# The first channel product of the last batch as seven half-size products for eight

## The chip, the cores and the metric

The kernel runs on one core of a Trainium2 chip. The metric is device time in microseconds (us) of one execution; the median of several runs is compared. The engines are named as in the profile: PE (TensorE), with PEld for its weight loads, DVE (VectorE), ACT (ScalarE), POOL (GpSimd) and SP (SyncE, which here issues DMAs). Matmuls write PSUM, eight banks of 128 partitions x 512 f32; only PE, ACT and DVE work on it here. All else lies in SBUF.

## The reference

Sliding-window attention with four sink tokens (batch 4, 8 heads, 768 tokens, head size 64), followed by a block that mixes tokens and channels (512 channels):

```python
x   = attention(q, k, v).transpose(0, 2, 1, 3).reshape(4, 768, 512)
a1  = alpha1 * x + beta1
tok = einsum("ts,bsd->btd", w_tok, a1)
u   = x + lam * tok
a2  = alpha2 * u + beta2
ch  = maximum(a2 @ w_ch1, 0) @ w_ch2        # 512 -> 2048 -> 512
out = u + lam * ch
```

The change touches `a2 @ w_ch1` of batch 3, the last one.

## The kernel before, in words

Work is in f16 with sums in f32. Each batch goes through attention (24 steps of head pairs and windows), token mixing (`tok`, six tiles of 128 tokens x 512 channels, each six matmuls of 512 columns, then a DVE add into x, which now holds u, L867, and a cast to f16 on ACT or POOL), a transpose of u by DMA (`uTx`: SP issues six DMA transposes, L919; then eight affines by alpha2 and beta2, one for each 128 channels and each half of the tokens, on ACT, L884, or DVE, L886), the first channel product and the second one. The attention of a batch is interleaved with the channel products of the one before it; batch 3's products at the end have nothing beside them but the end of batch 2's.

**First channel product** (`mlp1`): h is made transposed, 2048 hidden channels as 16 tiles of 128, 768 tokens as 2 chunks of 384. Each of the 32 tiles `h_chunk_fi` is one PSUM bank (pool d, four banks) and four matmuls of 384 columns (L940) over the 512 input channels; then one relu into hT, on ACT (L946) or DVE (L948).

**Second channel product** (`prod`, batches 1 to 3): here the 2x2 block product of hT (tokens by hidden halves) with w_ch2 (hidden by channel halves) already is done as seven products P1 to P7 for eight, by Winograd's form of Strassen's method. Four sums of w_ch2 (L972) and four sums of hT (`h_sums`, S1 to S4, L998 to L1001) are made ahead. A product's tile of 128 tokens x 256 channels is eight matmuls of 256 columns (L1057). The results are gathered by DVE in x (L1070) and, where two outputs share a sum, in an SBUF tile pt (L1088), which is added to x in 512 columns (L1096) and in 256 (L1093). At the end x goes out by DMA (L1076).

**What sets the order.** Every piece of work is a task. Four tables, written out, hold for all tasks their order (ORDER), engine (ENGINES), the buffer that each tile gets from its pool (HOMES) and some idle matmuls (IDLES); `Plan.emit` (L54 to L74) issues the tasks in this order. Each engine then runs its own instructions strictly in that order, and waits by semaphores are set where a tile is written after others have read or written it, for the tile as a whole. Of PSUM's eight banks four are single (pool d); pool S is two tiles of two banks, used in attention for scores. Pool E (six SBUF tiles) holds the exponentials, n16 (four) the f16 copies of q and k, wst (four) w_ch2 on its way in; all these are free by batch 3's end.

Of the kernel before, what the change touches and what calls it, by code (L numbers as in the profile page):

```python
# [77 lines left out]
def kernel(  # L78
# [119 lines left out]
    for r in range(NR):  # L198
# [91 lines left out]
    )  # L290
    ENGINES = (
        "3313134433443333444444444444444433334443111211211212021212021203331121211210210200201210"
# [7 lines left out]
        "2032121312121312104210421040001210421042104000121212120212121212121202120202021202121202"  # L300
        "0202020112120202020212020112021212121211111212121212121213121112131214214214210214214044"
        "4404404404433333304040404043404040202010121203012121312010121213320103212131203012121312"
        "0321213321213121042104210410002104213421341010202021202120212120212020202020212020212120"
        "202020112020212021202020112020210202142141111212121212121211121112131210210210214210210"
    )
    HOMES = (
        "145602340010102001213310200221013302203140101100511203013044215120821000003331a501103130"
# [4 lines left out]
        "0021102210121102223200511310123320031102032021035337572302312010320101420152002210101311"  # L312
        "162103012154110041003020b005101119102307200030023123011223130032122313100100121232070302"
        "1202002102135312330203"
    )
    IDLES = (
        (46, 0, 67), (90, 1, 25), (109, 3, 2), (166, 1, 4), (162, 0, 1),
# [528 lines left out]
    pch = {}  # L846

    def tok(p, b, ti):
        pt = Buf("S" if (b, ti) == (0, 5) else "d", None, None, f"tok{b}_{ti}")
        bx = x[b, ti]  # L850

        def bank():
            return pt.t[:, 0] if pt.kind == "S" else pt.t
        bu = u16[b, ti] = Buf("u16", None, None, f"u16_{b}_{ti}")
        hs = [xh[b, si] for si in range(NR)]

        def mm(sis):
            def f(e):
                for si in sis:
                    nc.tensor.matmul(  # L860
                        bank(), wtokT[:, si, ti * P : (ti + 1) * P], hs[si].t,
                        start=(si == 0), stop=(si == NR - 1))
            return f

        def ua(e):
            xf = bx.t.rearrange("p h d -> p (h d)")
            nc.vector.tensor_add(xf, xf, bank())  # L867
# [64 lines left out]
    def mlp1(p, b, chk, fi):  # L932
        if fi == 0:
            hT[b, chk] = Buf("hT", None, None, f"hT{b}_{chk}")
        bh, bu = hT[b, chk], uT[b, 0]
        ph = Buf("d", [P, NTOK], FP32, f"h{b}_{chk}_{fi}")

        def mm(e):
            for c in range(NC):
                nc.tensor.matmul(  # L940
                    ph.t, w1f[:, c, fi * P : (fi + 1) * P],
                    bu.t[:, c, chk * NTOK : (chk + 1) * NTOK], start=(c == 0), stop=(c == NC - 1))

        def relu(e):
            if e == ACT:
                nc.scalar.activation(bh.t[:, fi, :], ph.t, AF.Relu)  # L946
            else:
                nc.vector.tensor_scalar_max(bh.t[:, fi, :], ph.t, 0.0)  # L948
# [261 lines left out]
    for b in range(B):  # L1210
        w0 = STEP * b
        if b == 0:
            seq = [("tok", ti) for ti in range(3)] + [("uT", 0, 0), ("uT", 0, 1)]
            seq += [("tok", ti) for ti in range(3, NR)]
            m1 = []
            for qd in range(4):
                for chk in range(2):
                    m1 += [("m1", chk, fi) for fi in range(4 * qd, 4 * qd + 4)]
            m1.insert(3, ("uT", 1, 0))
            m1.insert(5, ("uT", 1, 1))  # L1220
        else:
# [3 lines left out]
        seq += m1  # L1225
        if b in STRASSEN:
# [4 lines left out]
            i = seq.index(("m1", 1, 8))  # L1231
# [21 lines left out]
        for i, (what, *args) in enumerate(seq):  # L1253
# [8 lines left out]
            {"tok": tok, "uT": uTp, "m1": mlp1, "m2": mlp2, "hs": h_sums, "pr": prod}[what](p, b, *args)  # L1262
            if b and what == "tok":
                uTx(p + 0.3, b, *args)
        if b + 1 == STRASSEN[0]:
# [68 lines left out]
```

## Time and profile before

| | |
|---|---|
| time, median of three runs | 254.27 us (254.3, 254.27, 253.2) |
| profiled execution, its own time | 253.3 us |
| its span | 251.5 us |
| matmul busy in the span | 245.2 us, 98% |
| DVE, ACT, POOL busy | 193.7, 131.5, 107.9 us |
| batch 3's first product on PE | 207.76 to 230.53, with a few tiles of the second product of batch 2 and 3 in between |
| batch 3's second product on PE | to 247.94 |

Of the profile this document shows: the share of busy time of each engine; the chain that ended last; groups of instructions ("L940 PE MATMUL h<-uT,w1f 128*128 128x384 f16 x512 | 89.3, 326 | 0.1" is: line, engine, operation, out<-in, shapes, how many | busy us, mean ns of one | idle us of the engine just before them, and what ended it); timelines (start us, us, engine, line, operation, out<-in, how many, and in brackets the idle time before with its releaser); and windows (for a stretch of time its length, then the busy time of each engine with its instructions, TensorE's granted clock as a share of full speed, the DMA share and GB/s). In a timeline a piece of several matmuls is listed up to its modelled end, which lies a little behind the start of the next. A line is that of the program's source; a helper's line (L155, L157: copies and casts) serves many places.

### The profile page before, as it was taken

The page shows a single profiled execution, that of the slowest core. Times are in us where ns is not written, and L with a number is a line of the kernel's source. Part 1 is how long each engine was busy: PE and PEld are TensorE (multiplying, and loading weights), DVE is VectorE, ACT ScalarE, POOL GpSimd, SP SyncE. Part 2 cuts the span into 40 slices and gives each one's busy share as a digit, 9 for nine tenths or more (in the row PEclk, how much of TensorE's full clock was granted, in tenths as well). Part 3 has the DMA queues.
Part 4 walks back from the last instruction along what each step waited for, and adds up shares of the span by engine and source line. Part 5 has one row for each costly group of instructions (what it writes and reads, how often), then busy time and mean ns, then how long its engine had stood idle before and what let it go on. Part 6 is the DMA issues. An engine that isn't in the chain of part 4 may idle for free.

```text
span 251.5 us, 5513 instructions
## 1 busy us (share of the span) xinstructions
PE 245.2 (98%) x2167; PEld 160.2 (64%) x2167; DVE 193.7 (77%) x401; ACT 131.5 (52%) x218; POOL 107.9 (43%) x126
## 2 busy tenths in 40 slices
PE   8899999999999999999999999999999999999994
PEld 7654655575555444566777676567677676567883
DVE  6898987778788976688889995677689985119883
ACT  2389935788985125687750545556660235543000
POOL 8728724986866516442872040065563130000010
PEclk9999999999999999999999999999999999999999
DMA  6999999999999997796489264420000147100006
GB/s 206 212 262 346 222 183 292 361 357 285 219 208 220 231 198 163 166 257 150 108 171 183 55 148 136 126 65 0 3 0 3 21 77 234 46 0 3 22 3 229
DMA packets 86129, 38.79 MB, mean 154 GB/s; under 512 B 73540, under 2 KB 80460, under 8 KB 86104
## 3 DMA queue, kind: packets, MB, share of 16 engines
q1 hardware_dynamic: 66976, 28.85, 48.2%
q10 hardware_dynamic: 15384, 6.32, 10.5%
q0 software_dynamic: 3744, 3.28, 8.3%
q8 instruction: 17, 0.28, 0.5%
q14 instruction: 8, 0.07, 0.1%
HBM read 29.91 MB, written 6.29 MB: 144 GB/s over the span
## 4 chain that ended last, share of the span: by engine, by line
PE 90%; ACT 4%; DVE 3%; issue 1%; DVEq 0%; ACTq 0%
PE h L940 32%; PE P L1057 22%; PE tok L860 12%; PE ch L1125 8%; PE pv L726 4%; PE S L625 4%; PE idle L148 2%; PE tp L515 1%; ACT wt L822 1%; ACT E L647 1%; DVE qkT L157 1%; PE S L620 1%; PE tp L512 1%; PE pv L719 1%; DVE lb_b L1175 1%
## 5 line engine op out<-in xcount | busy, mean ns | idle before, releaser
L940 PE MATMUL h<-uT,w1f 128*128 128x384 f16 x512 | 89.3, 326 | 0.1
L940 PEld LDWEIGHTS <-w1f 128*128 128x128 f16 x512 | 48.4, 98 | 31.9 <-issue 2.0
L946 ACT ACTIVATE hT<-h 128x384 f16<-128x384 f32 x77 | 36.7, 492 | 34.5 <-PE h L940 30.7
L948 DVE TENSOR_SCALAR hT<-h 128x384 f16<-128x384 f32 x51 | 27.4, 552 | 23.7 <-PE h L940 23.3
L1057 PEld LDWEIGHTS <-hT 128*128 128x128 f16 x408 | 39.3, 98 | 7.2 <-DVE hT L1000 0.7
L647 ACT ACTIVATE E<-S 128x1024 f16<-128x1024 f32 (+1 forms) x39 | 37.9, 1002 | 6.8 <-PE S L625 5.7
L770 POOL TENSOR_TENSOR tm<-x,la_b 128x512 f32<-128x512 f32 x18 | 24.7, 1372 | 22.2 <-DVE xh L773 12.0
L860 PE MATMUL tok<-xh,wtokT 128*128 128x512 f16 x144 | 33.2, 379 | 0.0
L1057 PE MATMUL P<-w2f,hT 128*128 128x256 f16 x216 | 26.8, 273 | 0.0
L155 ACT CAST u<-x 128x512 f16<-128x512 f32 x17 | 10.3, 616 | 28.3 <-DVE x L867 27.3
L1093 POOL TENSOR_TENSOR x<-x,pt 128x256 f32<-128x256 f32 x4 | 3.8, 961 | 46.0 <-DVE pt L1088 46.0
L1070 DVE TENSOR_TENSOR x<-x,P 128x256 f32<-128x256 f32 x45 | 18.0, 417 | 6.8 <-PE P L1057 6.0
L1057 PE MATMUL P<-w2s,hT 128*128 128x256 f16 x192 | 23.3, 273 | 0.0
L860 PEld LDWEIGHTS <-wtokT 128*128 128x128 f16 x144 | 13.8, 98 | 14.8 <-issue 0.2
L1125 PE MATMUL ch<-w2f,hT 128*128 128x512 f16 x96 | 22.7, 379 | 0.0
L752 DVE TENSOR_TENSOR x<-pv,rec 128x256 f32<-128x256 f32 x48 | 20.4, 425 | 1.7
L155 ACT CAST n<-nat 128x768 f16<-128x768 f32 x20 | 16.2, 830 | 7.9 <-DMA out_dram<-x 4.8
L867 DVE TENSOR_TENSOR x<-x,tok 128x512 f32<-128x512 f32 x24 | 16.0, 681 | 4.5 <-PE tok L860 4.3
L726 PEld LDWEIGHTS <-E 128*128 128x128 f16 x328 | 15.2, 97 | 4.9 <-issue 1.1
L726 PE MATMUL pv<-vfs,E 128*128 128x65 f16 x328 | 17.7, 193 | 0.0
L587 POOL TENSOR_SCALAR_AFFINE_SELECT E<-E 128x512 f16<-128x512 f16 x12 | 8.8, 753 | 17.9 <-ACT E L647 17.9
L157 POOL CAST vfs<-vnat 128x512 f16<-128x512 f32 x18 | 13.5, 752 | 4.3 <-PE pv L726 4.2
(133 smaller groups left out, 340.1 us busy)
## 6 DMA issues: line engine op xcount, KB each, us to landing
wst_w<-in_moe_w_ch_dram SPq DMA_DIRECT2D x8, 512.0 KB, 7.4
nat<-in_q_dram SPq DMA_DIRECT2D x10, 384.0 KB, 4.3
nat<-in_k_dram SPq DMA_DIRECT2D x10, 384.0 KB, 8.1
vnat<-in_v_dram SPq DMA_DIRECT2D x14, 256.0 KB, 6.2
out_dram<-x SPq DMA_DIRECT2D x12, 256.0 KB, 3.4
wtn<-in_moe_w_tok_dram SPq DMA_DIRECT2D x6, 384.0 KB, 4.8
out_dram<-x ACTq DMA_DIRECT2D x9, 256.0 KB, 4.3
w1f<-in_moe_w_ch_dram POOLq DMA_DIRECT2D x4, 512.0 KB, 10.2
```

The costliest lines, as they stand in the source:

```text
L155: nc.scalar.copy(o, i)
L647: nc.scalar.activation(eT.t, pS.t[:, :, 0 : n * w].rearrange("p e (i w) -> p e i w", i=n), AF.Exp, scale=scale)
L726: nc.tensor.matmul(po.t[:, hl, :], eT.t[:, e_, off + i, c : c + P], vf[j][:, h, :], start=(r < 2 and n == 0), stop=(n == len(parts) - 1 an ...
L752: nc.vector.tensor_mul(bx.t[:, 4 * G : 4 * G + 4, :], po.t[:, :, 0:D], rec.t.to_broadcast([P, 4, D]))
L770: engine[e].tensor_mul(bt.t, bx.t.rearrange("p h d -> p (h d)"), la1_b)
L860: nc.tensor.matmul(bank(), wtokT[:, si, ti * P : (ti + 1) * P], hs[si].t, start=(si == 0), stop=(si == NR - 1))
L940: nc.tensor.matmul(ph.t, w1f[:, c, fi * P : (fi + 1) * P], bu.t[:, c, chk * NTOK : (chk + 1) * NTOK], start=(c == 0), stop=(c == NC - 1))
L946: nc.scalar.activation(bh.t[:, fi, :], ph.t, AF.Relu)
L948: nc.vector.tensor_scalar_max(bh.t[:, fi, :], ph.t, 0.0)
L1057: nc.tensor.matmul(pc.t, hh[:, nt * P : (nt + 1) * P], w(fi), start=(first and n_ == 0), stop=(n_ == HF - 1), skip_group_check=True)
L1070: nc.vector.tensor_add(row(bx)[:, cols], row(bx)[:, cols], pc.t)
L1125: nc.tensor.matmul(pc.t, bh.t[:, fi, nt * P : (nt + 1) * P], w2f[:, fi, :], start=(fi == 0), stop=(fi == NF - 1))
```

## The change

For batch 3 alone (HPAIR) `mlp1` is replaced by eight units `mlp1_pair`, i = 0 to 7. The hidden channels are taken in two halves (tile i and tile k = i + 8), the input channels in two halves, the tokens in two chunks, so that a unit makes the four h tiles (i, k by chunk 0, 1) by seven products of two matmuls of 384 columns:

- P1, P2: w_ch1's own blocks by u's own blocks; P3: sum S4 of w_ch1 by u; P4: w_ch1's block by T4; P5, P6, P7: S1 by T1, S2 by T2, S3 by T3, where S1 to S4 are sums and differences of w_ch1's four blocks (`w1_sums`, four pieces each, 16 DVE instructions of 128 x 2 x 256, in f16, in the wst tiles) and T1 to T4 those of u's (`u_sums`, four DVE instructions of 128 x 768, in the n16 tiles).
- P1 goes into a bank of a pair tile hA (pool S; units 0 and 1 share hA_0, 2 and 3 hA_1, then 4 and 5 hA_0, 6 and 7 hA_1). Copy k1 takes it to the bank hB, where P2 is added by matmul, and relu r11 makes tile (i, 0). P6 is added onto P1 in hA; copy k2 takes that to SBUF (hU). P7 is added in hA; P5, in a bank hE, is copied to SBUF (k5, hV); add a22 = hA + hV and a clip at zero in place (r22) make (k, 1). P4 is added in hA and relu r21 makes (k, 0). P3 is added onto P5 in hE; add a12 = hE + hU and clip r12 make (i, 1).

So a unit has nine evacuations and clips where four relus were. Copies and relus are on ACT or DVE, adds on DVE, ten clips on DVE and six on POOL. In the tables besides: three relus of batch 2 (h_0_5, h_0_6, h_1_8) go from DVE to ACT; batch 3's eight affines of u are all on ACT (five before); batch 3's six token mixing tiles run one behind the other on PE ahead of batch 2's P6, P5 and P3 tiles (between them before), two of them in pool S's tiles (before one, batch 0's last); the order of the DMA transposes on SP is 1, 0, 2, 4, 3, 5 (before 2, 0, 1, 4, 5, 3); five of the six adds of pt into x of batch 3's second product go from DVE to POOL.

What it does to the order, at two places. First DVE, where batch 3's first product begins: x_1 and x_2 are results of batch 2, hT_0 and hT_1 the two chunks of batch 3's h. Before:

```order
L1070 TENSOR_TENSOR x_1_1884<-x_1_1884,P_2_1_3311 128x256
L948 TENSOR_SCALAR hT_0_3345<-h_0_7_3368 128x384
L948 TENSOR_SCALAR hT_0_3345<-h_0_9_3375 128x384
L886 TENSOR_SCALAR uT_3237<-uT_3237,ab_70 128x384
L948 TENSOR_SCALAR hT_0_3345<-h_0_2_3382 128x384
L886 TENSOR_SCALAR uT_3237<-uT_3237,ab_70 128x384
L948 TENSOR_SCALAR hT_0_3345<-h_0_4_3443 128x384
```

and with the change (the number after hA_, hB_, hE_, hU_, hV_ is that of the tile or unit):

```order
L1202 TENSOR_TENSOR x_2_2012<-x_2_2012,P_2_2_3314 128x256
L1046 TENSOR_SCALAR hT_0_3377<-hB_2_3395 128x384
L1051 TENSOR_TENSOR hT_1_3430<-hA_0_3335,hV_1_3411 128x384
L1056 TENSOR_SCALAR hT_1_3430<-hT_1_3430 128x384
L1051 TENSOR_TENSOR hT_1_3430<-hA_0_3335,hV_0_3432 128x384
L1051 TENSOR_TENSOR hT_1_3430<-hE_1_3404,hU_1_3407 128x384
L1056 TENSOR_SCALAR hT_1_3430<-hT_1_3430 128x384
L1051 TENSOR_TENSOR hT_1_3430<-hE_0_3425,hU_0_3402 128x384
L157 COPY hU_3_3461<-hA_1_3352 128x384
L1051 TENSOR_TENSOR hT_1_3430<-hA_1_3352,hV_2_3463 128x384
```

Relus, each of a bank of its own, are replaced by adds, clips and copies that read the two hA tiles, which the next products write. Second, the end of the program: DVE from the last sums of hT on. Before:

```order
L1001 TENSOR_TENSOR hT_0_3345<-hT_0_3345,hT_s_3616 128x1536
L1070 TENSOR_TENSOR x_2_2856<-x_2_2856,P_3_2_3647 128x256
L1070 TENSOR_TENSOR x_4_3055<-x_4_3055,P_3_1_3618 128x256
L1088 TENSOR_TENSOR pt_1_3572<-pt_1_3572,P_3_1_3697 128x256
L1088 TENSOR_TENSOR pt_2_3667<-pt_2_3667,P_3_2_3687 128x256
L1096 TENSOR_TENSOR x_5_3116<-x_5_3116,pt_2_3667 128x512
L1070 TENSOR_TENSOR x_3_2959<-x_3_2959,P_3_0_3708 128x256
L1070 TENSOR_TENSOR x_5_3116<-x_5_3116,P_3_2_3719 128x256
L1093 TENSOR_TENSOR x_1_2766<-x_1_2766,pt_1_3572 128x256
L1096 TENSOR_TENSOR x_4_3055<-x_4_3055,pt_1_3572 128x512
```

and with the change:

```order
L1133 TENSOR_TENSOR hT_0_3377<-hT_0_3377,hT_s_3699 128x1536
L1220 TENSOR_TENSOR pt_0_3633<-pt_0_3633,P_3_0_3724 128x256
L1220 TENSOR_TENSOR pt_1_3605<-pt_1_3605,P_3_1_3714 128x256
L1202 TENSOR_TENSOR x_4_3075<-x_4_3075,P_3_1_3690 128x256
L1202 TENSOR_TENSOR x_5_3136<-x_5_3136,P_3_2_3702 128x256
L1202 TENSOR_TENSOR x_3_2979<-x_3_2979,P_3_0_3756 128x256
L1220 TENSOR_TENSOR pt_2_3644<-pt_2_3644,P_3_2_3767 128x256
L1202 TENSOR_TENSOR x_4_3075<-x_4_3075,P_3_1_3778 128x256
L1202 TENSOR_TENSOR x_5_3136<-x_5_3136,P_3_2_3789 128x256
L1202 TENSOR_TENSOR x_0_2703<-x_0_2703,P_3_0_3756 128x256
```

with these now at the end of POOL's order, the six adds behind the six clips:

```order
L1056 TENSOR_SCALAR hT_1_3430<-hT_1_3430 128x384 x6
L1228 TENSOR_TENSOR x_3_2979<-x_3_2979,pt_0_3633 128x512
L1225 TENSOR_TENSOR x_1_2781<-x_1_2781,pt_1_3605 128x256
L1228 TENSOR_TENSOR x_4_3075<-x_4_3075,pt_1_3605 128x512
L1225 TENSOR_TENSOR x_0_2703<-x_0_2703,pt_0_3633 128x256
L1228 TENSOR_TENSOR x_5_3136<-x_5_3136,pt_2_3644 128x512
L1225 TENSOR_TENSOR x_2_2871<-x_2_2871,pt_2_3644 128x256
```

DVE keeps the adds that read PSUM; those of pt (x_0 to x_5, pt_0 to pt_2) have gone from between them to POOL.

The diff, cut to its core (the tables ORDER, ENGINES and HOMES change from the places of these tasks on):

```diff
...
-        pt = Buf("S" if (b, ti) == (0, 5) else "d", None, None, f"tok{b}_{ti}")
+        pt = Buf("S" if (b, ti) in ((0, 5), (3, 3), (3, 4)) else "d", None, None, f"tok{b}_{ti}")
...
+    HPAIR = (3,)
...
+    def w1_sums(p):
...
+        for s, sub_, i0, i1, need in (("S1", 0, a21, a22, None), ("S2", 1, "S1", a11, "S1"),
+                                      ("S3", 1, a11, a21, None), ("S4", 1, a12, "S2", "S2")):
+            for g in range(4):
+                f = slice(256 * g, 256 * g + 256)
...
+    def u_sums(p, b):
...
+        for s, i0, i1, need, parts in (("T1", b12, b11, None, c11 + c12), ("T2", b22, "T1", "T1", c22),
+                                       ("T3", b22, b12, None, c12 + c22), ("T4", b21, "T2", "T2", c21)):
...
+    def mlp1_pair(p, b, i):
...
+            for g in range(2):
+                pairs[b, g] = Buf("S", None, None, f"hA{b}_{g}")
...
+        bA = pairs[b, i % 4 // 2]
+        bB = Buf("d", [P, NTOK], FP32, f"hB{b}_{i}")
+        bE = Buf("d", [P, NTOK], FP32, f"hE{b}_{i}")
+        bU = Buf("E", [P, NTOK], FP32, f"hU{b}_{i}")
+        bV = Buf("E", [P, NTOK], FP32, f"hV{b}_{i}")
+        A = lambda: bA.t[:, i % 2, 0:NTOK]
...
+        m1 = mm("P1", A, lambda n_: w(n_, i), lambda n_: tok_(n_, 0), True, True, w1_ + half, [bA, bu])
+        k1 = add(p, {ACT: 395, DVE: 480}, lambda e, k=f"k1.{i}": copy(e, bB.t, A()), [m1], [bA, bB])
+        m2 = mm("P2", B_, lambda n_: w(2 + n_, i), lambda n_: tok_(2 + n_, 0), False, True, w1_ + half + [k1], [bB, bu])
+        done["h", b, 0, i] = relu("r11", c11, B_, [m2], [bB, h0])
+        m6 = mm("P6", A, lambda n_: sums("S2", n_), lambda n_: uD[b, "T2"].t[:, n_], False, True,
+                [k1, done["aS2", g], done["uT2", b]], [bA, aS["S2"], uD[b, "T2"]])
+        k2 = add(p, {ACT: 395, DVE: 480}, lambda e, k=f"k2.{i}": copy(e, bU.t, A()), [m6], [bA, bU])
+        m5 = mm("P5", E_, lambda n_: sums("S1", n_), lambda n_: uD[b, "T1"].t[:, n_], True, True,
+                [done["aS1", g], done["uT1", b]], [bE, aS["S1"], uD[b, "T1"]])
+        m7 = mm("P7", A, lambda n_: sums("S3", n_), lambda n_: uD[b, "T3"].t[:, n_], False, True,
+                [k2, done["aS3", g], done["uT3", b]], [bA, aS["S3"], uD[b, "T3"]])
+        k5 = add(p, {ACT: 395, DVE: 480}, lambda e, k=f"k5.{i}": copy(e, bV.t, bE.t), [m5], [bE, bV])
+        a22 = plus("a22", c22, A, lambda: bV.t, [m7, k5], [bV, bA, h1])
+        done["h", b, 1, k_] = clip("r22", c22, [a22], [h1])
+        m4 = mm("P4", A, lambda n_: w(2 + n_, k_), lambda n_: uD[b, "T4"].t[:, n_], False, True,
+                w1_ + [a22, done["uT4", b]], [bA, uD[b, "T4"]])
+        done["h", b, 0, k_] = relu("r21", c21, A, [m4], [bA, h0])
+        m3 = mm("P3", E_, lambda n_: sums("S4", n_), lambda n_: tok_(2 + n_, 1), False, True,
+                [k5, done["aS4", g]] + [done["uT", b, 1, c] for c in range(NC)], [bE, aS["S4"], bu])
+        a12 = plus("a12", c12, E_, lambda: bU.t, [m3, k2], [bE, bU, h1])
+        done["h", b, 1, i] = clip("r12", c12, [a12], [h1])
...
+        if b in HPAIR:
+            m1 = [("us",)] + [("hp", i) for i in range(NF // 2)]
...
```

More of the change, by code (lines that the diff above doesn't have):

```diff
@@ L953, in mlp1, with f_ @@
         done["h", b, chk, fi] = add(p + 0.1, {ACT: 395, DVE: 480}, relu, [a], [ph, bh])
+    HPAIR = (3,)
+    aS = {}
+    uD = {}
+    pairs = {}
+    def w1_sums(p):
+        a11, a12 = w1f[:, 0:2, 0 : DFF // 2], w1f[:, 2:4, 0 : DFF // 2]
+        a21, a22 = w1f[:, 0:2, DFF // 2 : DFF], w1f[:, 2:4, DFF // 2 : DFF]
+        for s in ("S1", "S2", "S3", "S4"):
+            aS[s] = Buf("wst", [P, 2, DFF // 2], FP16, f"w1{s}")
+        for s, sub_, i0, i1, need in (("S1", 0, a21, a22, None), ("S2", 1, "S1", a11, "S1"),
+                                      ("S3", 1, a11, a21, None), ("S4", 1, a12, "S2", "S2")):
+            for g in range(4):
+                f = slice(256 * g, 256 * g + 256)
+                def f_(e, s=s, sub_=sub_, i0=i0, i1=i1, f=f):
+                    r0, r1 = [aS[z].t if isinstance(z, str) else z for z in (i0, i1)]
+                    op = engine[e].tensor_sub if sub_ else engine[e].tensor_add
+                    op(aS[s].t[:, :, f], r0[:, :, f], r1[:, :, f])
+                done["a" + s, g] = add(
+                    p, {POOL: 2500, DVE: 700}, f_,
+                    [done["w1", i] for i in range(4)] + ([done["a" + need, g]] if need else []),
+                    [aS[s]] + ([aS[need]] if need else []), port=True)
@@ new lines, in u_sums, with f_ @@
+    def u_sums(p, b):
+        bu = uT[b, 0]
+        b11, b12 = (lambda: bu.t[:, 0:2, 0:NTOK]), (lambda: bu.t[:, 0:2, NTOK:S])
+        b21, b22 = (lambda: bu.t[:, 2:4, 0:NTOK]), (lambda: bu.t[:, 2:4, NTOK:S])
+        for s in ("T1", "T2", "T3", "T4"):
+            uD[b, s] = Buf("n16", [P, 2, NTOK], FP16, f"uD{b}{s}")
+        c11, c12, c21, c22 = [[(chk, c), (chk, c + 1)] for c in (0, 2) for chk in range(2)]
+        for s, i0, i1, need, parts in (("T1", b12, b11, None, c11 + c12), ("T2", b22, "T1", "T1", c22),
+                                       ("T3", b22, b12, None, c12 + c22), ("T4", b21, "T2", "T2", c21)):
+            def f_(e, s=s, i0=i0, i1=i1):
+                r0, r1 = [uD[b, z].t if isinstance(z, str) else z() for z in (i0, i1)]
+                engine[e].tensor_sub(uD[b, s].t, r0, r1)
+            done["u" + s, b] = add(
+                p, {DVE: 500, POOL: 1900}, f_,
+                [done["uT", b, chk, c] for chk, c in parts]
+                + ([done["u" + need, b]] if need else []),
+                [uD[b, s], bu] + ([uD[b, need]] if need else []), port=True)
@@ new lines, in mlp1_pair, with mm, f_, tok_ @@
+    def mlp1_pair(p, b, i):
+        bu = uT[b, 0]
+        if i == 0:
+            for chk in range(2):
+                hT[b, chk] = Buf("hT", None, None, f"hT{b}_{chk}")
+            for g in range(2):
+                pairs[b, g] = Buf("S", None, None, f"hA{b}_{g}")
+        h0, h1 = hT[b, 0], hT[b, 1]
+        k_ = i + NF // 2
+        bA = pairs[b, i % 4 // 2]
[4 more added lines that the diff above has]
+        A = lambda: bA.t[:, i % 2, 0:NTOK]
+        w = lambda c, f: w1f[:, c, f * P : (f + 1) * P]
+        g = i // 2
+        def mm(name, o, ws, xs, start, stop, after, uses):
+            def f_(e, name=f"{name}.{i}"):
+                for n_ in range(2):
+                    nc.tensor.matmul(o(), ws(n_), xs(n_), start=start and n_ == 0, stop=n_ == 1,
+                                     skip_group_check=True)
+            return add(p, {PE: 326}, f_, after, uses)
+        def tok_(c, chk):
+            return bu.t[:, c, chk * NTOK : (chk + 1) * NTOK]
+        def sums(s, n_):
+            return aS[s].t[:, n_, i * P : (i + 1) * P]
+        def relu(name, o, pt, after, uses):
+            def f_(e, name=f"{name}.{i}"):
+                if e == ACT:
+                    nc.scalar.activation(o(), pt(), AF.Relu)
+                else:
+                    nc.vector.tensor_scalar_max(o(), pt(), 0.0)
+            return add(p, {ACT: 395, DVE: 480}, f_, after, uses)
+        def plus(name, o, i0, i1, after, uses):
+            def f_(e, name=f"{name}.{i}"):
+                nc.vector.tensor_add(o(), i0(), i1())
+            return add(p, {DVE: 480}, f_, after, uses)
+        def clip(name, o, after, uses):
+            def f_(e, name=f"{name}.{i}"):
+                engine[e].tensor_scalar_max(o(), o(), 0.0)
+            return add(p, {POOL: 600, DVE: 250}, f_, after, uses, port=True)
+        w1_ = [done["w1", z] for z in range(4)]
+        B_ = lambda: bB.t
+        E_ = lambda: bE.t
+        c11, c21 = (lambda: h0.t[:, i, :]), (lambda: h0.t[:, k_, :])
+        c12, c22 = (lambda: h1.t[:, i, :]), (lambda: h1.t[:, k_, :])
+        half = [done["uT", b, 0, c] for c in range(NC)]
+        m1 = mm("P1", A, lambda n_: w(n_, i), lambda n_: tok_(n_, 0), True, True, w1_ + half, [bA, bu])
[19 more added lines that the diff above has]
+        done["h", b, 1, i] = clip("r12", c12, [a12], [h1])
@@ L1230 @@
             seq += two("P1", "P2")
-            i = seq.index(("m1", 1, 8))
+            i = seq.index(("pr", "P1", 0) if b in HPAIR else ("m1", 1, 8))
             seq[i:i] = [("hs", "S3")]
```

20 lines of the change are left out of this document (12 added, 8 removed), and 54 rows, old and new, of the table ORDER.

## The prediction

> **What bounds the kernel now.** I read the page first: the busy shares, the chain that ended last, and the costliest groups.
>
> ```profile
> span 251.5 us, 5513 instructions
> PE 245.2 (98%) x2167; PEld 160.2 (64%) x2167; DVE 193.7 (77%) x401; ACT 131.5 (52%) x218; POOL 107.9 (43%) x126
> PE 90%; ACT 4%; DVE 3%; issue 1%; DVEq 0%; ACTq 0%
> L940 PE MATMUL h<-uT,w1f 128*128 128x384 f16 x512 | 89.3, 326 | 0.1
> L940 PEld LDWEIGHTS <-w1f 128*128 128x128 f16 x512 | 48.4, 98 | 31.9 <-issue 2.0
> ```
>
> TensorE (PE) is busy 98% of the span and is 90% of the chain, so time is won by taking matmuls away and lost by making TensorE wait. The first channel product (L940, all four batches) starts its 512 matmuls with 0.1 us of idle time in all: there is no wait to remove, only work. Next, TensorE's timeline where batch 3's first product runs, and the busy times of the engines from there on.
>
> ```profile
> start us, us, engine line op out<-in xcount [idle before <-releaser]
> 207.76 1.46 PE L940 MATMUL h<-uT,w1f 128*128 128x384 f16 x8
> 209.06 1.04 PE L1057 MATMUL P<-w2f,hT 128*128 128x256 f16 x8
> 209.94 19.01 PE L940 MATMUL h<-uT,w1f 128*128 128x384 f16 x116
> ...
> 208.61 0.49 ACT L946 ACTIVATE hT<-h 128x384 f16<-128x384 f32 x1 [1.98 <-PE h L940]
> ...
> core 0: us, PE busy (x) PEld busy (x) DVE busy (x) ACT busy (x) POOL busy (x), PEclk, DMA share, GB/s
> 192.80:205.90 13.10, 13.10 (x87) 8.16 (x86) 11.71 (x21) 3.34 (x6) 2.08 (x4) 1.00 0.21 40
> 210.00:230.50 20.50, 20.50 (x133) 12.83 (x132) 8.11 (x15) 10.06 (x22) 0.00 (x0) 1.00 0.18 68
> 231.20:248.00 16.80, 16.74 (x153) 14.75 (x151) 13.90 (x29) 0.86 (x2) 1.23 (x1) 1.00 0.18 60
> ```
>
> From 210.00 to 230.50 TensorE never stops, while DVE and ACT work only 8.11 and 10.06 us: each group of four matmuls has its own bank and one relu. A matmul takes 0.1625 us there (the piece from 210.10 to 228.95 has 116), and half a group's cost in the new form, two matmuls, is 0.325.
>
> **What is removed.** 128 matmuls become 8 units of 7 products of 2: 112. 16 x 0.1625 = **2.60 us** less TensorE work.
>
> **Work that hides.** The 16 sums of w_ch1 (128x512 elements a partition) cost what these do:
>
> ```profile
> L972 DVE TENSOR_TENSOR w2f<-w2f 128x512 f16<-128x512 f16 x2 | 0.8, 418 | 0.0
> 154.24 1.02 DVE L948 TENSOR_SCALAR hT<-h 128x384 f16<-128x384 f32 x2 [1.27 <-PE h L940]
> 156.19 1.21 DVE L948 TENSOR_SCALAR hT<-h 128x384 f16<-128x384 f32 x2 [0.93 <-PE h L940]
> 161.72 0.56 DVE L948 TENSOR_SCALAR hT<-h 128x384 f16<-128x384 f32 x1 [1.73 <-PE h L940]
> 179.27 0.18 DVE L751 RECIPROCAL rec<-pv 128x4 f32<-128x4 f32 x1 [1.15 <-PE pv L726]
> 160.09 0.49 ACT L946 ACTIVATE hT<-h 128x384 f16<-128x384 f32 x1 [2.44 <-PE h L940]
> ```
>
> Twelve stand in the order between about 152.9 and 161.7 (12 x 0.418 = 5.0): 3.93 of DVE's idle time plus two relus gone to ACT (2 x 0.55) is 5.0. Four (1.7) stand ahead of 179.27: 1.15 idle and one moved relu. ACT had 2.44 idle for the relus it gets. I take 0; without that cover, at most the 1.4 to 1.7 us of one such group reaches TensorE once. The six tok tiles now run in one piece, which brings the transposes of u forward. No matmul is added by it, so 0.
>
> **The chain of a unit.** This is what the change adds to the path. Seven products go through one bank of a pair tile hA in turn, and after most of them ACT or DVE must copy or add before the next may be written. hA is two banks shared by two units, and the waits are by the whole tile: P4.1 (product 4 of unit 1) waits for the last reader of unit 0's bank too. The prices:
>
> ```profile
> L946 ACT ACTIVATE hT<-h 128x384 f16<-128x384 f32 x77 | 36.7, 492 | 34.5 <-PE h L940 30.7
> L1070 DVE TENSOR_TENSOR x<-x,P 128x256 f32<-128x256 f32 x45 | 18.0, 417 | 6.8 <-PE P L1057 6.0
> L867 DVE TENSOR_TENSOR x<-x,tok 128x512 f32<-128x512 f32 x24 | 16.0, 681 | 4.5 <-PE tok L860 4.3
> L948 DVE TENSOR_SCALAR hT<-h 128x384 f16<-128x384 f32 x51 | 27.4, 552 | 23.7 <-PE h L940 23.3
> 11.32 0.95 DVE L157 COPY qkT<-tp 128x768 f16<-128x768 f16 x1
> 12.32 0.27 PE L148 MATMUL idle<-warm 128*128 128x128 f16 x2 [0.36 <-DVE qkT L157]
> ```
>
> A group's last matmul to its reader's start: 208.61 - (207.76 + 4 x 0.1625) = 0.20. An ACT copy or relu of 384: 0.49. A DVE add of 384, midway between 0.417 and 0.681, or a DVE copy: 0.55. Back to TensorE: 12.32 - 12.27 = 0.05. So a step with n other product groups in between makes TensorE wait 0.74 - 0.325n after ACT, 0.80 - 0.325n after DVE: hidden from n = 3, 0.42 or 0.48 at n = 1, 0.09 or 0.15 at n = 2. Walked through the new order of TensorE with these:
>
> - P4.3 (behind the copy of P1.6) and P7.4 (behind the copy of P6.5) have n = 1: 0.42 each. P7.5, behind the add of P7.4: 0.48. P7.3, behind the add of P7.2, n = 2: 0.15. P4.2, behind the add of P7.3 with P1.4 in between: 0.10.
> - P4.1: after P7.0, DVE does unit 1's add, its clip (0.28, between the 0.18 of L751, a row of next to no data, and the 0.417 of L1070; either end moves the sum by 0.14 at most) and unit 0's add: 0.20 + 0.55 + 0.28 + 0.55 + 0.05, less three groups (0.975) = 0.66. P7.2, behind an add and a copy on DVE: 0.20 + 0.55 + 0.55 + 0.05 - 0.975 = 0.38. P1.4, behind two ACT copies (pitch 0.44): 0.37. P7.7, behind P6.7's copy and P7.6's add: 0.35.
> - P6.0 needs u's second difference. Chunk 1's four affines stand behind the first copy on ACT (206.36):
>
> ```profile
> 204.22 1.90 ACT L884 ACTIVATE uT<-uT,ab 128x384 f16<-128x384 f16 x3 [5.23 <-DMA uT<-u]
> ```
>
> At 0.605 each (three in 1.90 with the last one's tail) they end at 209.4, the difference (0.55) at 209.95; TensorE is there at 205.83 + 3.93 = 209.76: 0.24.
>
> These ten sum to 3.57. The load is no bound: nine evacuations a unit are 14 to 18 us for each of ACT and DVE in some 24.
>
> **The tail.** Six adds of a pt tile go to POOL in one piece; DVE did five of them.
>
> ```profile
> L1096 POOL TENSOR_TENSOR x<-x,pt 128x512 f32<-128x512 f32 x1 | 1.4, 1389 | 12.4 <-DVE pt L1088 12.4
> 200.05 0.73 POOL L1093 TENSOR_TENSOR x<-x,pt 128x256 f32<-128x256 f32 x1 [9.29 <-DVE pt L1088]
> 243.57 1.23 POOL L1093 TENSOR_TENSOR x<-x,pt 128x256 f32<-128x256 f32 x1 [36.67 <-DVE pt L1088]
> 245.16 2.78 PE L1057 MATMUL P<-w2f,hT 128*128 128x256 f16 x24
> ```
>
> The first starts behind P6's first tile (0.20 + 0.42 for the DVE add + 0.05), the fifth (x_5) ends 3 x 1.39 + 2 x 0.73 = 5.63 later, a DVE add (0.05 + 0.42 + 0.05) frees the bank of the last but one product: 6.82, and with DVE's queue 0.04 late, 6.86. TensorE fills seven product tiles of 0.87 (a third of 2.62, less the last one's overhang) in it: 6.09. It waits **0.77**; at 1.23 for the short adds, 1.8. No f16 sum of DVE is running by then. By the Trainium skill, page "SBUF — State Buffer", section "SBUF: two separate sides", a VectorE instruction with two SBUF inputs and a GpSimd one that reads SBUF lock each other out. Here that would touch only POOL's clips of the pair stage, since the DVE adds of the tail have one input in PSUM. The trace has a row that agrees, below, and the rule's own result is the last rival.
>
> **Sum.** 3.57 + 0.77 - 2.60 = **+1.74 us**. The profiled execution took 253.3 (span 251.5 and 1.8 around it), so 255.0 there; the median shown is 254.27, 1.0 higher, so **256.0**. What follows TensorE's last matmul (an add and the last output transfer) is the same.
>
> **Rivals.**
> - *No change, 254.3.* P6.0, P4.1 and the tail's wait (1.67 together) hang on when an engine gets there, not on a fixed n. If DVE and ACT run ahead there, 4.34 - 1.67 = 2.67 is left, as much as is saved. For it: both engines had half their time free in this stage. Against: the three adds on POOL at 1.39 are a fixed length.
> - *Faster, 252.4.* The order alternates products of two to four units; if this covers every step (a hand-over 0.4 shorter than 0.20 + 0.05, which is enough where n is 1 and which the modelled matmul ends could hide), only the tail's wait stays: 0.77 - 2.60 = -1.83. For it: the second channel product, likewise banks with reads in between, has 16.74 busy of 16.80 us in the window from 231.20. Against: it has 0.87 us per group to hide a read, this one 0.325.
> - *The change doesn't shorten TensorE's work*: the smaller groups cost more than 0.325, say by a weight load exposed at each of the 56. The trace has 64% for weight loads beside 98%, each 98 ns under 162; I give this nothing of its own.
> - *Much slower, 257.5.* POOL's clips and DVE's f16 work hold each other up:
>
> ```profile
> 189.49 1.27 POOL L770 TENSOR_TENSOR tm<-x,la_b 128x512 f32<-128x512 f32 x1
> 189.85 1.72 DVE L999 TENSOR_TENSOR hT<-hT 128x1536 f16<-128x1536 f16 x1
> 233.47 0.95 DVE L1000 TENSOR_TENSOR hT_s<-hT,hT 128x1536 f16<-128x1536 f16 x1
> ```
>
> Beside POOL a sum took 1.72, alone 0.95: 0.77 more. Two such delays on DVE ahead of an add that TensorE waits for are 1.5: 253.3 + 1.74 + 1.5 = 256.5, against the median 257.5.
>
> **How the numbers follow.** Chances: my sum 0.50 (own range 255.0 to 257.2, from the waits at n = 1 half hidden to the short POOL adds at 1.23), no change 0.25, faster 0.16, much slower 0.09. A measurement of this kernel tells about 0.5% (1.27 us) from no change: slower means above 255.54, which holds for seven tenths of the first case and for the last, and some of the no-change case's edge: 0.49. Faster means below 253.0: most of the third and a little of the second, 0.17; same 0.34. The range is 252.6 to 258.0: up to the last rival and a little beyond, down to the faster one's upper half.
>
> **What would show it.** Right: TensorE's window from its first P1 to its last P4 has about 18.2 us of pair products and some 3.5 us of idle time, put down to ACT copies and DVE adds, in waits of 0.1 to 0.7; the granted clock stays 1.00; TensorE has one wait of 0.5 to 1 us before one of its last three product tiles, behind a DVE add that itself waited for POOL. Wrong: waits under 1.5 us in the pair stage (then the hand-over is smaller than 0.25), no wait in the tail (then POOL's adds are shorter or earlier), a stall before the first P1 or in batch 2 where the sums stand, or the span's difference lying outside these places.

## The result, and the profile after

Nine runs of each: 255.07 us after, 253.67 before (the three shown first were 253.2 to 254.3), ratio 1.0053 with a 95% interval of 1.0037 to 1.0068. The change made the kernel **1.40 us slower**; the prediction was 1.74 slower, 256.0 in all. The profiled execution took 254.82 (before 253.3). From the page after:

```profile
span 252.9 us, 5576 instructions
PE 244.9 (97%) x2151; PEld 159.4 (63%) x2151; DVE 205.6 (81%) x436; ACT 138.2 (55%) x232; POOL 120.4 (48%) x137
```

There are 16 matmuls fewer, and the span is 1.4 us longer, so TensorE waits. A window of the kernel after shows the stage (columns as in the prediction):

```profile
core 0: us, PE busy (x) PEld busy (x) DVE busy (x) ACT busy (x) POOL busy (x), PEclk, DMA share, GB/s
210.00:229.50 19.50, 17.26 (x99) 9.38 (x97) 14.92 (x33) 11.42 (x26) 5.37 (x5) 1.00 0.09 35
```

Between 210.0 and 229.5, where it never stopped before, TensorE now has 2.24 us without a matmul, and that is after each group's modelled end, which lies 0.16 behind the moment at which the next could start. The waits are better read from start to start in TensorE's timeline of the kernel after. Each pair of rows here is a group and the one that waited; a group of two takes 0.325.

```profile
208.23 1.91 PE L1189 MATMUL P<-w2f,hT 128*128 128x256 f16 x16
210.10 0.81 PE L1031 MATMUL hA<-uD3T,w1S 128*128 128x384 f16 x4
...
213.75 0.49 PE L1031 MATMUL hE<-uT,w1S 128*128 128x384 f16 x2
214.74 0.48 PE L1031 MATMUL hA<-uD3T,w1f 128*128 128x384 f16 x2 [0.50 <-DVE hT L1051]
...
216.03 0.49 PE L1031 MATMUL hA<-uD3T,w1f 128*128 128x384 f16 x2
216.86 0.48 PE L1031 MATMUL hA<-uD3T,w1S 128*128 128x384 f16 x2 [0.34 <-DVE hU L157]
...
217.50 0.49 PE L1031 MATMUL hA<-uT,w1f 128*128 128x384 f16 x2
218.06 0.48 PE L1031 MATMUL hA<-uD3T,w1S 128*128 128x384 f16 x2
218.67 0.48 PE L1031 MATMUL hA<-uT,w1f 128*128 128x384 f16 x2
219.26 0.49 PE L1031 MATMUL hA<-uD3T,w1f 128*128 128x384 f16 x2
...
221.53 0.49 PE L1031 MATMUL hE<-uD3T,w1S 128*128 128x384 f16 x2
222.25 0.49 PE L1031 MATMUL hA<-uD3T,w1f 128*128 128x384 f16 x2 [0.23 <-ACT hB L155]
...
224.20 0.81 PE L1031 MATMUL hA<-uD3T,w1S 128*128 128x384 f16 x4
225.25 0.48 PE L1031 MATMUL hA<-uD3T,w1S 128*128 128x384 f16 x2 [0.24 <-ACT hU L155]
225.57 0.49 PE L1031 MATMUL hE<-uD3T,w1S 128*128 128x384 f16 x2
226.45 0.48 PE L1031 MATMUL hA<-uD3T,w1S 128*128 128x384 f16 x2 [0.39 <-DVE hT L1051]
...
228.73 0.49 PE L1031 MATMUL hE<-uT,w1S 128*128 128x384 f16 x2
229.45 0.49 PE L1031 MATMUL hA<-uD3T,w1S 128*128 128x384 f16 x2 [0.24 <-DVE hT L1051]
...
246.47 3.04 PE L1189 MATMUL P<-w2f,hT 128*128 128x256 f16 x24
```

The row at 214.74 follows one that starts at 213.75 and lasts 0.325: a wait of 0.67. All of them, with the forecast behind the stroke:

| before | measured / forecast | before | measured / forecast |
|---|---|---|---|
| P6.0 | 0.13 / 0.24 | P4.2 | 0.27 / 0.10 |
| P7.1 | 0.07 / 0 | P4.3 | 0.39 / 0.42 |
| P4.1 | 0.67 / 0.66 | P7.4 | 0.40 / 0.42 |
| P7.2 | 0.50 / 0.38 | P7.5 | 0.55 / 0.48 |
| P7.3 | 0.23 / 0.15 | P7.7 | 0.39 / 0.35 |
| P1.4 | 0.28 / 0.37 | last product tile but one (tail) | 0.26 / 0.77 |

That is 3.88 in the pair stage (forecast 3.57) and 0.26 in the tail, 4.14 against 4.34. The tail, in POOL's and DVE's timelines of the kernel after:

```profile
242.01 1.27 POOL L1228 TENSOR_TENSOR x<-x,pt 128x512 f32<-128x512 f32 x1 [10.11 <-DVE pt L1220]
245.83 1.26 POOL L1228 TENSOR_TENSOR x<-x,pt 128x512 f32<-128x512 f32 x1
247.13 0.84 DVE L1202 TENSOR_TENSOR x<-x,P 128x256 f32<-128x256 f32 x2 [0.84 <-POOL x L1228]
```

The five adds end at 247.09, 5.08 after the first began, and DVE's add starts 0.04 later: the chain is the one forecast, and shorter than its 5.63.

For comparing stretches I use one measure below: **from batch 3's first token mixing matmul to the end of TensorE's last one** (start of the last piece, plus 0.109 for each of its matmuls, plus a wait inside it). Before: 245.16 + 2.62 - 192.82 = 54.96. After: 246.47 + 2.62 + 0.26 - 193.04 = 56.31, so +1.35. The waits of 4.14 less the matmuls' 2.60 are 1.54. The other 0.2 are small waits that the kernel before has in this stretch and the changed one has not: 0.13 ahead of the piece at 206.89 (the one before it starts at 205.89 and has eight matmuls of 0.109), and 0.05 in the first token mixing piece. Up to the start of this stretch the two traces differ by a constant 0.2 to 0.3 from 50 us on, ahead of every changed instruction.

### The profile page after: what moved, and what is told of

It reads as the page before. It is cut to its first block, busy times and chain, and to the rows that moved or that the text cites. A ratio compares the mean times of both kernels' runs of the same rounds, so it can differ in the third digit from the quotient of the medians.

```text
span 252.9 us, 5576 instructions
## 1 busy us (share of the span) xinstructions
PE 244.9 (97%) x2151; PEld 159.4 (63%) x2151; DVE 205.6 (81%) x436; ACT 138.2 (55%) x232; POOL 120.4 (48%) x137
## 4 chain that ended last, share of the span: by engine, by line
PE 87%; ACT 4%; DVE 4%; issue 2%; POOL 1%; POOLq 0%; DVEq 0%; ACTq 0%
PE h L947 24%; PE P L1189 21%; PE tok L867 12%; PE ch L1257 8%; PE hA L1031 4%; PE pv L733 4%; PE S L632 4%; PE idle L148 2%; PE hE L1031 1%; PE tp L522 1%; ACT wt L829 1%; DVE hT L1051 1%; ACT E L654 1%; PE tp L519 1%; DVE qkT L157 1%
## 5 line engine op out<-in xcount | busy, mean ns | idle before, releaser
L947 PE MATMUL h<-uT,w1f 128*128 128x384 f16 x384 | 68.0, 326 | 0.1
L947 PEld LDWEIGHTS <-w1f 128*128 128x128 f16 x384 | 35.9, 98 | 24.0 <-issue 2.0
L953 ACT ACTIVATE hT<-h 128x384 f16<-128x384 f32 x58 | 27.9, 493 | 21.2 <-PE h L947 17.6
L955 DVE TENSOR_SCALAR hT<-h 128x384 f16<-128x384 f32 x38 | 20.4, 552 | 8.2 <-PE h L947 7.8
L1189 PE MATMUL P<-w2s,hT 128*128 128x256 f16 x192 | 22.6, 272 | 0.0
L157 POOL CAST u<-x 128x512 f16<-128x512 f32 x7 | 4.9, 714 | 27.1 <-DVE x L874 18.1
L1056 POOL TENSOR_SCALAR hT<-hT 128x384 f16<-128x384 f16 x6 | 7.1, 1184 | 19.3 <-DVE hT L1051 19.3
## 6 DMA issues: line engine op xcount, KB each, us to landing
vnat<-in_v_dram SPq DMA_DIRECT2D x14, 256.0 KB, 6.2
out_dram<-x SPq DMA_DIRECT2D x12, 256.0 KB, 3.0
out_dram<-x ACTq DMA_DIRECT2D x9, 256.0 KB, 4.9
```

Of the source, the lines that this page charges most:

```text
L947: nc.tensor.matmul(ph.t, w1f[:, c, fi * P : (fi + 1) * P], bu.t[:, c, chk * NTOK : (chk + 1) * NTOK], start=(c == 0), stop=(c == NC - 1))
L1189: nc.tensor.matmul(pc.t, hh[:, nt * P : (nt + 1) * P], w(fi), start=(first and n_ == 0), stop=(n_ == HF - 1), skip_group_check=True)
```

## The experiments

Theory A: TensorE's waits are steps (hand-over to ACT or DVE, copy or add, hand-over back) that the order does not cover with other product groups, and a step counts for the whole two-bank tile. Rivals: the waits belong to the form with its nine evacuations on loaded engines; a group of two matmuls is dearer than half of four; the waits are by the bank.

**Another order of the same tasks (e1_spaced).** Only ORDER, from batch 3's token mixing on.

```diff
 plan.emit(ORDER, ENGINES, HOMES, IDLES)
-    ORDER = (... the changed kernel's)
+    ORDER = (... the tasks from tok3_0 on in an order with at least three groups between
+             a product and the one that waits for its reader)
```

> Only the order table is changed, from batch 3's token mixing on: the same tasks, engines and buffers, but on TensorE enough other product groups stand between a product and the one that waits for its reader (three or more of 0.325 us after each 0.20 + 0.48 to 0.56 + 0.05 step). Theory A (the waits are steps of a chain that the order does not cover): TensorE has no waits left in the pair stage or the tail, the 3.9 + 0.3 us seen in the changed kernel go, and the full 2.60 us of removed matmuls remain: 2.6 below the kernel before, about 251.1, 4.0 below the changed kernel. Rival B (the waits come with the seven-product form, by nine evacuations a unit on two loaded engines): no order removes them, at most 1 us goes, 254 or more. Rival C (a group of two matmuls simply costs more than 0.325): the time between waits grows, no gain from an order.

Measured 253.0, ratio to before 0.9969 (0.9955 to 0.9984): 0.7 faster than before instead of 2.6. TensorE's stretch tells more: 243.80 + 2.62 - 193.60 = 52.82, 3.5 below the changed kernel and 2.14 below before. So an order does remove the waits, which fells rivals B and C for TensorE: the matmuls cost what they were said to. Of the 2.14, 1.3 were given back behind TensorE. (The profiled execution also reaches the stretch 0.8 later than the one before. The instructions ahead of it are the changed kernel's, which starts it at 193.04, so this is not the order's doing; over the traces of this case, e5_twice's aside, the start lies between 192.8 and 193.6.) The transfers of the result, before and here, and here two last adds on DVE:

```profile
244.58 4.19 ACTq L1076 DMA_DIRECT2D out_dram<-x  x6
244.93 1.52 SPq L1076 DMA_DIRECT2D out_dram<-x  x2
```

```profile
244.82 1.15 SPq L1203 DMA_DIRECT2D out_dram<-x  x2
246.20 2.36 ACTq L1203 DMA_DIRECT2D out_dram<-x  x5
243.14 0.74 DVE L1197 TENSOR_TENSOR x<-x,P 128x256 f32<-128x256 f32 x2
```

Before, ACT issued six from 244.58 on; here five within 2.4 us from 246.20 on, and the span ends 5.0 us behind the last matmul (251.4 against 246.4) instead of 3.7 (251.5 against 247.8). My order was made for TensorE alone and let the transfers bunch up at the end. The adds were not late for it: the two in the last row are the last ones of x_4 and x_3, done at 243.88, but in ACT's order the transfers of both stand behind that of x_1, whose last add TensorE releases only at 245.75. No run moves the transfers alone, so the 1.3 are put down to them by these rows. About 0.7 us of small waits were left as well; they are explained three experiments on.

**The tail's adds back on DVE (e2_tail).**

```diff
-        ... pt adds x_3, x_1, x_4, x_0, x_5 of batch 3: engine 3 (POOL)
+        ... the same five: engine 1 (DVE); x_2's stays on POOL
```

> The changed kernel with five of the six adds of pt back on DVE, as they were before the change; the order is kept. Theory A (the fifth POOL add holds back the DVE add that frees the last product's bank): the wait of 0.26 us in the tail goes, nothing else moves, 0.26 us faster than the changed kernel, 254.8. Rival: DVE, which has the last adds to do as well, gets late itself and gives the wait back, 255.1 or more.

Measured 254.85, ratio to before 1.0050 (1.0030 to 1.0070). By the times alone this can't be told from the changed kernel (1.0053). By the trace the wait is gone: the last piece of TensorE is 24 matmuls in 2.78 us instead of 3.04, and the stretch is 56.05, 0.26 shorter. POOL's adds were worth a quarter of a microsecond.

**Copies of twice the length (e3_copies).**

```diff
+        def twice(e, o, i0):
+            for _ in range(2 if e == ACT else 1):
+                copy(e, o, i0)
-        k1 = add(p, ..., lambda e, ...: copy(e, bB.t, A()), [m1], [bA, bB])     # k2, k5 likewise
+        k1 = add(p, ..., lambda e, ...: twice(e, bB.t, A()), [m1], [bA, bB])
```

> The changed kernel with each of the copies k1, k2 and k5 that ACT makes issued twice, one behind the other (the second writes the same values): about 0.43 us more for each step that ends in an ACT copy, none for steps that end in a DVE add. Theory A (each wait is the step's length less the groups in between): the waits behind ACT copies grow by 0.4 each (P4.3 and P7.4 to about 0.85, P1.4 to about 1.1), those behind DVE adds alone stay (P7.5 at 0.5), steps that were covered show up, and TensorE's waits sum to about 7.7 instead of 4.1: 3.6 us slower than the changed kernel, 258.7. Rival (the waits are a fixed cost of switching accumulation groups, or of a bank): ACT had 40% of its time free here, and under 1 us is lost.

Measured 258.94 (expected 258.7), ratio 1.0213 (1.0194 to 1.0231). The rows that answer to P4.3, P7.4, P7.5 and P7.7:

```profile
225.62 0.48 PE L1036 MATMUL hA<-uD3T,w1f 128*128 128x384 f16 x2 [0.72 <-ACT hB L155]
229.30 0.48 PE L1036 MATMUL hA<-uD3T,w1S 128*128 128x384 f16 x2 [0.91 <-ACT hU L155]
230.50 0.49 PE L1036 MATMUL hA<-uD3T,w1S 128*128 128x384 f16 x2 [0.39 <-DVE hT L1056]
234.01 0.49 PE L1036 MATMUL hA<-uD3T,w1S 128*128 128x384 f16 x2 [0.75 <-DVE hT L1056]
```

The idle time before the first two grew from 0.23 and 0.24 by 0.49 and 0.67, a copy's length or a little more; that before the third, which follows a DVE add, is the same 0.39. The fourth grew too, from 0.24 to 0.75, though it is put down to a DVE add; the next experiment shows why. The waits are the steps' length, on an engine that in the changed kernel was itself free 40% of the time.

**Other neighbours in a tile (e4_remap).** Units 0 and 2 share a tile, and 1 and 3, in place of 0 and 1, 2 and 3. The order is untouched; in HOMES the entry of hA_1 moves to unit 1, now its first user.

```diff
-        bA = pairs[b, i % 4 // 2]
+        bA = pairs[b, i % 2]
-        A = lambda: bA.t[:, i % 2, 0:NTOK]
+        A = lambda: bA.t[:, i % 4 // 2, 0:NTOK]
```

> The changed kernel with the pair tiles shared by other units: units 0 and 2 share one two-bank tile, 1 and 3 the other (4 and 6, 5 and 7 likewise), instead of neighbours; order, engines and the number of banks are as they were. Each unit still has a bank of its own among four. Theory A (a wait is set by the whole two-bank tile, so a unit waits for its neighbour's readers too): most waits go, since neighbours in the order no longer share a tile; left are P6.0's 0.27, new ones of 0.34 to 0.44 at P1.3 and P6.3, about 0.4 near P7.5 and P6.7 and the tail's 0.25, in sum 1.7 instead of 4.1: 2.3 us faster than the changed kernel, 252.7. Rival B (the waits are by the bank, and the chain of one unit is what takes the time): no bank changes hands in another way, so nothing moves, 255.1.

Measured 253.79, ratio 1.0010 (0.9997 to 1.0023): 1.3 us faster than the changed kernel, no change from before. Rival B had nothing moving, so the sharing does cost. But half of what A promised didn't come: by starts, about 3.05 us of waits are left, and 1.7 were expected. One of them, with what lies behind it, in the timelines of TensorE, DVE and ACT:

```profile
218.32 0.48 PE L1031 MATMUL hA<-uT,w1f 128*128 128x384 f16 x2 [0.20 <-DVE hT L1051]
217.71 0.56 DVE L1051 TENSOR_TENSOR hT<-hA,hV 128x384 f16<-128x384 f32 x1 [0.46 <-ACT hT L1044]
217.18 0.49 ACT L1044 ACTIVATE hT<-hA 128x384 f16<-128x384 f32 x1
```

TensorE waits for a DVE add (unit 2's), and this add stood idle for 0.46 us until an ACT relu had ended, which reads the other bank of the tile (unit 0's) and writes the other tile of h (hT_0, the add hT_1). The add's own product was done by about 217.2. So two **readers** of a pair tile, one on ACT and one on DVE, wait for each other: not only a write to the tile counts. The releasers in brackets are inferred from semaphores, so these are waits of the program as it is built; that the chip itself asks for them isn't shown. (It is not so for every tile and engine: hT, in SBUF, is read by TensorE and DVE at the same time in the changed kernel, from 231.62 on.) The changed kernel has it as well, ahead of the wait at P7.7, in ACT's and DVE's timelines of the kernel after:

```profile
228.33 0.48 ACT L155 COPY hU<-hA 128x384 f32<-128x384 f32 x1 [1.36 <-PE hA L1031]
228.84 0.56 DVE L1051 TENSOR_TENSOR hT<-hA,hV 128x384 f16<-128x384 f32 x1 [0.38 <-ACT hU L155]
```

Unit 6's add stands until the copy from unit 7's bank has ended, 0.38 us in which DVE is free; this is why P7.7's wait grew with the copies in e3_copies, where the same add stood for 0.89. In e1_spaced the largest of the waits left, 0.23 before P7.6 and 0.18 before P4.6, hang on a copy by ACT that stood behind a DVE reader of the same tile. Theory A is mended by that rule. Counted again with it (a count made after these runs, which this document does not show), this kernel should wait 3.5, e1_spaced 0.8 and the changed kernel 4.2, where 3.05, about 0.65 (its stretch against the waitless one below) and 4.14 were measured.

**Sums twice over (e5_twice).** Is the w_ch1 sums' place really free?

```diff
-                    op(aS[s].t[:, :, f], r0[:, :, f], r1[:, :, f])
+                    for _ in range(2):
+                        op(aS[s].t[:, :, f], r0[:, :, f], r1[:, :, f])
```

> The changed kernel with each of the 16 sums of w_ch1 issued twice, one behind the other (the same values): 5.0 us more of DVE work between 152.9 and 161.7 and 1.7 ahead of 179.3, where DVE was busy 8.10 of 8.80 and 7.53 of 9.30 us. Theory A (the sums cost nothing because they just fill DVE's idle time there): the second set has no cover, the relus of batch 2 come late and TensorE waits for their banks, 1.65 us at the first relus and 0.9 at the next group of sums: 2.5 us slower than the changed kernel, 257.6. Rival (DVE has slack enough there): under 0.5 us.

Measured 265.04, ratio 1.0451 (1.0428 to 1.0475): 10 us slower than the changed kernel, four times what was expected. TensorE's timeline and the windows of this kernel:

```profile
168.51 0.96 PE L947 MATMUL h<-uT,w1f 128*128 128x384 f16 x4 [2.55 <-DVE x L1203]
...
core 0: us, PE busy (x) PEld busy (x) DVE busy (x) ACT busy (x) POOL busy (x), PEclk, DMA share, GB/s
166.00:168.00 2.00, 0.00 (x0) 0.00 (x0) 1.97 (x4) 0.00 (x0) 2.00 (x3) 1.00 0.00 0
170.00:172.00 2.00, 2.00 (x11) 1.00 (x10) 1.02 (x3) 0.62 (x1) 0.00 (x0) 0.50 0.00 0
174.00:176.00 2.00, 2.00 (x32) 1.83 (x29) 1.65 (x6) 1.26 (x4) 0.41 (x1) 1.00 0.08 24
...
189.01 4.45 PE L947 MATMUL h<-uT,w1f 128*128 128x384 f16 x16 [2.27 <-DVE x L759]
190.00:192.00 2.00, 2.00 (x8) 0.91 (x6) 0.96 (x3) 0.00 (x0) 1.26 (x1) 0.50 0.00 0
```

The sums had no slack: the second set put DVE late by several us, which answers the question. What I hadn't counted on is the clock. After TensorE had stood still for 2.55 us it was granted half its clock, 0.50 from 170 to 172 and full again by 174; the same after 2.27 us at 189 (16 matmuls in 4.45, which is 2.6 at full clock). By the Trainium skill, page "TensorE: Matmul & The Clock Gate", section "What's actually happening", the clock falls to half after an idle window of some 3.4 us. The half is what the trace has, but here pauses of 2.3 and 2.6 us were enough. The waits of 0.7 us at most in the changed kernel left it at 1.00. The 10 us are not split further: the pauses named make up 6.1 with three smaller ones, half clock perhaps 3.2 (an estimate: some 3.2 us at half speed after each of the two, half of it lost), and the rest is open.

**Both rules in an order (e6_both).** A new order up to the pair stage's last product that also keeps ACT and DVE off one tile, the tail's order as in the changed kernel, so that the transfers leave in time.

```diff
-    ORDER, ENGINES = (... the changed kernel's)
+    ORDER = (... anew from tok3_0 to the last P4; behind it as it was)
+    ENGINES = (... all clips on DVE, five pt adds of the tail on DVE, two pt adds of batch 2 on DVE,
+               two casts of u on ACT, two affines on DVE, 15 copies and relus between ACT and DVE,
+               three of batch 2's output transfers between the queues of SP and ACT)
```

> The changed kernel, with a new order up to the last product of the pair stage and, from there on, the order of the changed kernel; all ten clips and the six that POOL had are on DVE; the six adds of pt in the tail are on DVE; some copies, relus and affines change places between ACT and DVE; buffers and pair tiles stay. The order is made with one rule more than e1_spaced had: ACT and DVE don't read the same two-bank tile at the same time, which is what left the waits in e1_spaced (0.2 before a P7, 0.2 before a P4) and in e4_remap. Theory A2 (that rule, the step's length and the output transfers issued as early as before account for all that e1_spaced lacked): no wait over 0.1 us in the pair stage, TensorE's last matmul 2.3 to 2.6 us earlier than in the kernel before, the end 3.5 us behind it as in the kernel before: 251.3 (2.4 faster than before). Rival (what e1_spaced lacked is lost in some other way, such as the last transfers sharing bandwidth whatever the order): 252.5 or more.

Measured **250.82**, ratio to before **0.9895** (0.9873 to 0.9917): 2.6 us faster than before and faster than either kernel. (One of the six adds of pt, x_2's, stayed on POOL.) Page and windows:

```profile
span 248.9 us, 5553 instructions
PE 243.2 (98%) x2151; PEld 159.6 (64%) x2151; DVE 207.5 (83%) x448; ACT 139.0 (56%) x235; POOL 104.5 (42%) x122
210.00:229.00 19.00, 19.00 (x128) 12.25 (x126) 17.18 (x45) 12.19 (x28) 0.00 (x0) 1.00 0.19 71
```

TensorE is busy all of 19.00 us with DVE at 90%, and nothing waits. The stretch is 242.80 + 2.62 - 193.25 = 52.17, 2.8 below before (16 matmuls are 2.60, and 0.2 are the small waits of the kernel before), and the end is 3.5 behind it (3.7 before). So the removed work is worth its full 2.6 us as soon as the waits are covered.

**POOL's clips again (e7_poolclip).** That kernel with the six clips back on POOL.

```diff
-        ... clips r12.0, r12.1, r12.2, r22.5, r12.5, r22.7: engine 1 (DVE)
+        ... the same: engine 3 (POOL)
```

> e6_both with the six clips (r12.0, r12.1, r12.2, r22.5, r12.5, r22.7) back on POOL, where the change had them; the order and all else stay. A clip takes 1.17 us on POOL and 0.25 on DVE, and nothing in the pair stage waits for them. Theory A (a clip on POOL costs only its own time on an engine that is idle): no wait on TensorE, 250.8 as e6_both, DVE 1.0 us less busy. Rival L (a DVE clip in f16, or a DVE sum of two SBUF tiles, stands still while POOL works on f16 in SBUF, as one row of e1_spaced suggests, in which three DVE clips took 1.04 us beside a POOL clip, for 0.59 when POOL is idle): DVE clips and sums beside the six POOL clips last up to 1.2 us, DVE's adds come late by 0.3 to 0.9 some three times and TensorE waits 0.5 to 1.5 us in all: 251.3 to 252.3.

Measured 250.95, ratio 0.9894 (0.9872 to 0.9917): the same as without, and TensorE waits nowhere in the stage. POOL and DVE do hold each other up in places, in the timelines of this kernel:

```profile
217.50 2.39 POOL L1051 TENSOR_SCALAR hT<-hT 128x384 f16<-128x384 f16 x2 [0.74 <-DVE hT L1046]
228.19 2.76 POOL L1051 TENSOR_SCALAR hT<-hT 128x384 f16<-128x384 f16 x2 [3.57 <-DVE hT L1046]
229.85 0.56 DVE L1051 TENSOR_SCALAR hT<-hT 128x384 f16<-128x384 f16 x1
```

Beside a DVE sum two POOL clips took 2.76, elsewhere 2.39; a DVE clip beside them 0.56 for 0.25. Two other DVE clips beside clips on POOL, at 219.28 and 228.61, took 0.25 and 0.26, as when alone. In e1_spaced it was more, three DVE clips in 1.04 (0.59 when POOL is idle):

```profile
219.92 1.04 DVE L1051 TENSOR_SCALAR hT<-hT 128x384 f16<-128x384 f16 x3
241.72 1.50 DVE L1128 TENSOR_TENSOR hT<-hT,hT_s 128x1536 f16<-128x1536 f16 x1
```

This agrees with the lock of the Trainium skill ("SBUF — State Buffer", section "SBUF: two separate sides") for sums with two SBUF inputs (the second row: 1.50 beside a POOL add, 0.95 otherwise), and for some of the DVE clips but not all. It costs a few tenths on DVE and reached TensorE nowhere in this kernel. Of rival L in this experiment the mechanism is right in part and the price is zero.

## Why the prediction was right

**What is removed, 2.60.** Right: without waits (e6_both) the stretch is 2.8 shorter than before, 2.6 by the 16 matmuls and 0.2 by small waits of the kernel before. That fells the rival by which smaller groups cost more.

**Work that hides, 0.** Right, and tightly so. With the sums DVE is busy 8.10 of 8.80 us between 152.9 and 161.7 (4.80 before), and TensorE's distance to the trace of before is 0.22 at 151 and 0.22 at 190. Twice the sums cost 10 us; the bound for a lost cover, 1.4 to 1.7 us once, was far too low, since it had one late relu in mind, and neither a queue of late work behind it nor the clock.

**The chain of a unit, 3.57 against 3.88.** The mechanism and the formula (0.74 - 0.325n, 0.80 - 0.325n) hold: n = 1 behind ACT gave 0.39 and 0.40 for 0.42, behind DVE 0.55 for 0.48; e3_copies confirms that the step's length is what counts. P7.2, P7.3 and P4.2 were 0.08 to 0.17 short in the sum, P6.0 0.11 over. The statement that waits are by the whole two-bank tile was right but incomplete: it also holds between two readers on ACT and DVE, which e4_remap brought out. In the changed kernel that makes the 0.07 before P7.1 and most of the 0.39 before P7.7. The sum had P7.7 nearly right because it put the copy of P6.7 and the add of P7.6 one behind the other, without giving this reason. In other orders the rule decides more.

**The tail, 0.77 against 0.26.** The term that was mis-sized. A POOL add of 512 columns takes 1.23 in a row there, not the 1.39 of the single row that I had, and one of 256 takes 0.68: 5.08 for 5.63. The wait came out below the 0.5 to 1 us that was named as its sign. The mechanism stands: e2_tail removes the wait.

**Sum and rivals.** +1.74 against +1.40 (stretch +1.35). The chain was 0.31 short, the tail 0.51 over, and the 0.2 of waits in the kernel before were not counted; that the total is nearer than the terms is partly luck. The 256.0 was 0.9 over, 0.6 of it because the median of the three runs then known, 254.27, lay above that of the nine. "No change" counted on the three waits that hang on arrival times being absent; they came to 0.13 + 0.67 + 0.26 of the 1.67. "Faster" needs every step covered; the order of the changed kernel doesn't, another order does. "Much slower" by DVE and POOL: they do hold each other up in places, at too low a price. What I had not priced at all is a POOL clip, 1.17 us; it is off TensorE's path.

## What to carry to other kernels

Saving TensorE a few per cent of its matmuls by chaining smaller products through PSUM paid here only once each step of the chain (0.25 of hand-overs plus about 0.5 for the copy or add) lay under other matmul groups; count the groups between, three of 0.325 us here, before moving any work. When two users share a tile that is tracked as one, an access of one engine may wait for another's, and between ACT and DVE on a PSUM tile here that held for reads too, so share it between users that are far apart in the order, and look for the second name in the row of the waiting engine. When an order is rearranged for the busiest engine, keep the output transfers as early as they were; otherwise the end gives the gain back.

## What the runs showed of the hardware that was not expected

- TensorE at half clock (granted 0.50) for some 3.2 us after pauses of 2.3 and 2.6 us; at 1.00 with pauses up to 0.7 (in the kernel with doubled copies 1.1).
- A clip of 128x384 in f16 in SBUF: 1.17 us on POOL, 0.25 on DVE.
- A POOL add of 128x512 in f32: 1.23 back to back in the tail, 1.67 (three in 5.02) where DVE summed f16 tiles beside it, and a DVE sum there 1.50 instead of 0.95.
